# The first batch of a fused retention and mixer kernel: another order of its loads, weight conversions and low parts

## The chip, the cores and the metric

The kernel runs on one core of one Trainium2 chip. The time is the device time of one execution in microseconds (us): 1366.73 is the median of three runs (1365.96 to 1366.76). One more execution was taken with the hardware profiler; it took 1366.12 us. All rows below are from that one.

## The reference

Three stages follow one another, in float32 and float64 (the weights of the mixers come as float64):

```python
# 8 batches, 8 heads, 576 positions, 64 channels a head
scores = scale * np.matmul(q, k.transpose(0, 1, 3, 2))
Dmat = np.where(rel >= 0, gamma[:, None, None] ** rel[None, :, :], 0.0)   # rel = i - j
x = np.matmul(scores * Dmat[None], v)            # heads joined: (8, 576, 512)

h = x.transpose(0, 2, 1) @ U @ V                 # U: 576 x 32, V: 32 x 576
u = x + h.transpose(0, 2, 1)
x = u + np.maximum(u @ w_ch1, 0.0) @ w_ch2       # w_ch1: 512 x 2048

xk = mu_k * x + (1.0 - mu_k) * x_prev            # x_prev: one token earlier
xr = mu_r * x + (1.0 - mu_r) * x_prev
k = np.maximum(xk @ w_k, 0.0)
out = sigmoid(xr @ w_r) * (k * k @ w_v)
```

The change touches the first stage of the first batch, the mixing with U and V, and the preparation of `w_ch1`.

## The kernel before, in words

**Retention.** It goes batch by batch, `NC` = 5 steps each, of 128 positions (the last of 64). A step works on one or two chunks of 64 positions. `scores(i)` multiplies q and k inside each chunk, `decay(i)` weighs the result on VectorE (tile `pm`), `own(i)` multiplies by v. `gain(i)` multiplies k by v to a state per head, `states(i)` adds it to the running state (tiles `w_1`, `w_2`, ...), and `inter(i)` multiplies q by that state. `from_state(i)` weighs the latter (tile `y`), and `leave(i)` adds the two parts into `xt`, the transposed x of the batch. `scale_k` weighs k on GpSimd before its use. Two PSUM pairs, `up` and `dn`, take all these small matmuls, 64 by 64 each. A batch's steps are numbered on: step 5 is the first of the second batch.

**Mixing.** `natural` transposes a step's x back on TensorE (`xn`), ScalarE copies it (`xs`), `low_rank` multiplies it by U (tile `ust`) into `gall`, and `low_rank_sum` makes from the sum over five steps a high part, a low part and a copy of the high part (tile `gt`). `mix` multiplies by V (tile `vst`, which holds a high part twice and a low part) and VectorE adds the product to `xt`. `mix_store` splits the result into high and low parts (`uh`, `ul`) for the dense products.

**Dense products.** `hidden_part` multiplies the mixed x by `w_ch1`. The matmuls are in fp32r, so both factors are split: high by high, high by low, low by high are summed, twelve matmuls of 128x512 for one product (tiles `h_0`, `h_1`, ...). The weight has four column quarters (`w1[0]` to `w1[3]`, in profile names `w_0` to `w_3`), and four products in turn use one quarter. `FIRST` and `FULL` say how many products follow each step.

**Weight conversions.** float64 arrives as two 32-bit words. `convert` makes of it in stages: a load; `down`, a scaling of the upper word on ScalarE (tile `ca`); `fill`, three VectorE instructions that join the words to a float32 (tile `cf`); `split`, a cast to the high part on ScalarE, then a subtraction for the low part, on GpSimd. A quarter is converted in four blocks of 128 rows.

**What sets the order.** Inside `manual_schedule` (L1074) each engine runs its instructions in the order in which the code issues them; an instruction that waits holds up everything behind it on that engine. The stages of conversions are put by hand: `place` takes a conversion's stages and files them in `early` under half-steps (2i is the first half of step i), and `stages` issues what is filed there. Loads go through SyncE's queue in the order of issue.

The lines in the rows: scores L801, `decay` L815, `inter` L834, `own` L853, `gain` L875, `states` L898 and L900, `from_state` L912, `leave` L929, `natural` L939 and L949, `low_rank` L960, `low_rank_sum` L975 to L982, `mix` L990 and L994, dense products L336 with their relu at L342, conversions L104 (ScalarE), L110, L114, L119 (VectorE), L127 (cast) and L128 (low part).

Of the kernel before, what the change touches and what calls it, by code (L numbers as in the profile page):

```python
# [19 lines left out]
DM = H * D  # L20
# [19 lines left out]
def retention_mixer_kernel(ctx: ExitStack, tc: tile.TileContext, io):  # L40
# [90 lines left out]

    waiting, going = [], []
# [13 lines left out]
    class Weight:  # L146
# [9 lines left out]
        def convert(self, pool, raw_pool):  # L156
            for k in range(4):
# [11 lines left out]
                waiting.append(convert(fetch, parts, 128, 512))  # L169


# [560 lines left out]
    with ExitStack() as st:  # L732
# [77 lines left out]
        def decay(i):  # L810
            b, p, cs = chunks(i)
            n = len(cs)
            t = up[i - 1] if i else up.pop(-1)
# [75 lines left out]
        def states(i):  # L889
# [12 lines left out]
            if i == 0:  # L902
                down.pop(-1)
# [31 lines left out]
        def natural(b, p):  # L935
            c0, n = CH[p]
            ps = bank("n", f"xn{b}_{p}")
# [33 lines left out]
        def low_rank_sum(b):  # L971
            gs = small(F32, "gs")[:32]
            gt = a2.tile([96, DM], F32R, tag="gt", name=f"gt{b}")
# [6 lines left out]
            eng = nc.gpsimd if b else nc.vector  # L980
            eng.tensor_tensor(gt[32:64], gs, gt[0:32].bitcast(F32), op=ALU.subtract)
            nc.scalar.copy(gt[64:96], gs)  # L982
            gst[b] = gt
# [3 lines left out]
        def mix(b, k, s):  # L987
# [3 lines left out]
                ps[:, :n], gst[b][:, k * 128:(k + 1) * 128], vst[:, o:o + n], start=True, stop=True  # L991
# [40 lines left out]
        def prep_u():  # L1032
            full, m = (NC - 1) * C, (NC - 1) * RANK
            n = S - full
            raw = []

            def fetch():
                raw.append(big.tile([128, NC * RANK], I64, tag="unit", name="uraw"))
                nc.sync.dma_start(
                    raw[0][:, :m].rearrange("p (c r) -> p c r", r=RANK),  # L1040
                    io["moe_U"][:full].rearrange("(c p) r -> p c r", p=C),
                )
                nc.sync.dma_start(raw[0][:n, m:], io["moe_U"][full:])
                return raw[0][:, :m]

            waiting.append(convert(fetch, lambda: (ust[:, :m], None), 128, m))
            waiting.append(convert(lambda: raw[0][:n, m:], lambda: (ust[:n, m:], None), n, RANK))

        def prep_v():
            q = S // 4
            vh, vl = small(F32R, "vh")[:, :q], small(F32R, "vl")[:, :q]

            def fetch():
                raw = big.tile([128, q], I64, tag="unit", name="vraw")
                for i in range(4):
                    nc.sync.dma_start(raw[32 * i:32 * i + 32], io["moe_V"][:, i * q:i * q + q])
                return raw

            def spread():
                for i in range(4):
# [43 lines left out]
        for w in w1:  # L1106
            w.convert(big, big)
# [434 lines left out]
```

## Time and profile before

| | us |
|---|---|
| median of three runs | 1366.73 |
| lowest, highest | 1365.96, 1366.76 |
| profiled execution | 1366.12 |
| its span (first to last instruction) | 1364.3 |

The page of the profile gives each engine's busy time as a share of the span, and the costliest groups of instructions. The trace behind it is asked by window (busy time of each engine in a stretch of time), by waits (what ended an engine's idle time) and as a timeline (one line for each instruction or run of like instructions, with its start). PE is TensorE, PEld its weight loads, DVE VectorE, ACT ScalarE, POOL GpSimd, SP SyncE. Times in a row are microseconds from the start of the span, unless they are marked ns. In brackets stands how long an engine waited before the instruction, and on what.

### The profile page before, as it was taken

Reading aid. Unit: us, or ns where it says so; the run is one execution under the profiler, and the core shown is the slowest. Engines: PE = TensorE matmul, PEld = TensorE weight load, DVE = VectorE, ACT = ScalarE, POOL = GpSimd, SP = SyncE. Lnnn points to the kernel's source line nnn. Section 1 sums busy time; section 2 is a strip of 40 time slices with the busy share of each in tenths; the row PEclk is TensorE's granted clock in tenths of the full one; section 3 lists DMA queues with packets and bytes.
Section 4 is the critical chain, followed back from the end, with each engine's and each line's share of the span. In section 5 each row is a group of like instructions: output and inputs, shape, how many; then the busy total and the mean of one; then the engine's idle time right before and its main releaser. Section 6 shows DMA issues by size and latency. Waiting matters only on the chain.

```text
span 1364.3 us, 25990 instructions
## 1 busy us (share of the span) xinstructions
PE 1336.9 (98%) x10296; PEld 1099.6 (81%) x10296; DVE 928.6 (68%) x1267; ACT 626.5 (46%) x1089; POOL 369.7 (27%) x301
## 2 busy tenths in 40 slices
PE   6899999999999999999999999999999999999998
PEld 4688887888877888788888888888888888888897
DVE  4893554441432266989798898697787787787753
ACT  4452434343333354544444544465465465465431
POOL 2351333323122155023221222203303303304212
PEclk8799999999999999999999999999999999999999
DMA  9576687886664557969788796786075175174271
GB/s 339 205 261 227 230 296 252 292 301 228 218 211 164 198 194 240 304 197 321 248 297 293 238 321 216 253 310 247 19 287 188 35 274 185 53 271 139 82 306 76
DMA packets 122763, 307.64 MB, mean 225 GB/s; under 512 B 15120, under 2 KB 27792, under 8 KB 122640
## 3 DMA queue, kind: packets, MB, share of 16 engines
q1 hardware_dynamic: 122640, 305.96, 64.4%
q8 instruction: 81, 1.33, 0.4%
q14 instruction: 42, 0.34, 0.1%
HBM read 214.69 MB, written 91.23 MB: 224 GB/s over the span
## 4 chain that ended last, share of the span: by engine, by line
PE 91%; DVE 3%; DMA 3%; issue 2%; ACT 1%; SPq 0%; POOL 0%; DVEq 0%; ACTq 0%
PE h L336 28%; PE v L1387 14%; PE ga L521 5%; PE gc L521 5%; PE gd L521 5%; PE kc L1291 4%; PE kd L1291 4%; PE ka L1291 4%; PE gb L521 3%; PE rd L1291 2%; PE kb L1291 2%; PE rc L1291 2%; PE ra L1291 2%; PE xn L939 2%; DMA rb<-hp 2%
## 5 line engine op out<-in xcount | busy, mean ns | idle before, releaser
L342 ACT ACTIVATE hs<-h 128x512 f32<-128x512 f32 x144 | 86.0, 598 | 233.1 <-PE h L336 228.1
L1343 POOL TENSOR_TENSOR vl<-m,vh 128x512 fp32r<-128x512 f32 (+1 forms) x40 | 47.6, 1192 | 310.2 <-ACT vh L1342 240.2
L815 DVE TENSOR_TENSOR pm<-up,dtab 128x512 f32<-128x512 f32 (+1 forms) x40 | 25.4, 634 | 113.0 <-PE up L801 107.2
L480 ACT CAST sbh<-rb 128x1024 fp32r<-128x1024 f32 x64 | 67.4, 1054 | 59.1 <-PE gd L521 47.4
L481 DVE TENSOR_TENSOR sbl<-rb,sbh 128x1024 fp32r<-128x1024 f32 x64 | 85.4, 1334 | 5.0 <-ACT sbh L480 4.8
L1387 PE MATMUL v<-vh,wv_0u 128*128 128x512 f32 x288 | 88.7, 389 | 0.0
L1387 PE MATMUL v<-vh,wv_1u 128*128 128x512 f32 x288 | 88.7, 389 | 0.0
L481 DVE TENSOR_TENSOR sal<-ra,sah 128x1024 fp32r<-128x1024 f32 (+1 forms) x64 | 65.5, 1023 | 21.5 <-PE gd L521 13.5
L480 ACT CAST sah<-ra 128x1024 fp32r<-128x1024 f32 (+1 forms) x64 | 53.5, 837 | 50.7 <-DVE ra L462 17.9
L763 POOL TENSOR_TENSOR kv<-kv,ktab 128x512 f32<-128x512 f32 (+1 forms) x40 | 42.1, 1051 | 102.3 <-DMA kv<-in_kv 93.2
L1343 POOL TENSOR_TENSOR vl<-c,vh 128x512 fp32r<-128x512 f32 (+1 forms) x40 | 62.2, 1573 | 25.9 <-ACT vh L1342 25.9
L1387 PEld LDWEIGHTS v<-vh,wv_1u 128*128 128x128 f32 x288 | 54.1, 188 | 11.2
L1387 PEld LDWEIGHTS v<-vh,wv_0u 128*128 128x128 f32 x288 | 53.9, 188 | 11.0
L994 DVE TENSOR_TENSOR xt<-mx,xt 128x256 f32<-128x256 f32 x64 | 28.7, 457 | 49.9 <-PE mx L990 49.9
L1342 ACT CAST vh<-m 128x512 fp32r<-128x512 f32 (+1 forms) x40 | 23.2, 579 | 75.3 <-DVE m L1341 75.3
L1387 PE MATMUL v<-vl,wv_0u 128*128 128x512 f32 x144 | 56.0, 389 | 0.0
L1387 PE MATMUL v<-vl,wv_1u 128*128 128x512 f32 x144 | 56.0, 389 | 0.0
L565 POOL TENSOR_TENSOR x<-x,ur 128x512 f32<-128x512 f32 x16 | 24.7, 1556 | 108.0 <-DVE x L561 76.7
L634 ACT ACTIVATE tp<-x2l,omu 128x511 f32<-128x511 f32 x72 | 51.0, 713 | 2.6 <-DMA x2l<-xb 2.6
L538 POOL TENSOR_TENSOR m<-m,ur 128x512 f32<-128x512 f32 x8 | 12.3, 1555 | 133.1 <-ACT m L535 133.1
L1341 DVE SCALAR_TENSOR_TENSOR m<-m 128x512 f32<-128x512 f32 (+1 forms) x40 | 44.8, 1119 | 1.4
L1291 PE MATMUL kc<-kht,wk 128*128 128x512 f32 (+1 forms) x160 | 45.5, 368 | 0.0
(289 smaller groups left out, 3828.2 us busy)
## 6 DMA issues: line engine op xcount, KB each, us to landing
wk<-keys SPq DMA_DIRECT2D x80, 512.0 KB, 5.9
hp<-hs SPq DMA_DIRECT2D x128, 256.0 KB, 3.0
rb<-hp SPq DMA_DIRECT2D x64, 512.0 KB, 5.6
wr<-gates SPq DMA_DIRECT2D x40, 512.0 KB, 7.7
qk<-in_qk SPq DMA_DIRECT2D x32, 512.0 KB, 6.2
kv<-in_kv SPq DMA_DIRECT2D x32, 512.0 KB, 6.9
ra<-hp SPq DMA_DIRECT2D x32, 512.0 KB, 6.8
ur<-ub SPq DMA_DIRECT2D x18, 512.0 KB, 6.1
```

Source lines behind the costliest of these rows:

```text
L336: nc.tensor.matmul(hps[t, f], w.part(lo, k, fo), u[k // 2][:, k % 2, :], start=(part == 0 and k == 0), stop=(part == 2 and k == KD - 1),)
L342: nc.scalar.activation(h, hps.pop((t, f)), AF.Relu)
L480: nc.scalar.copy(hi_, src)
L481: nc.vector.tensor_tensor(lo_, src, hi_.bitcast(F32), op=ALU.subtract)
L521: nc.tensor.matmul(group[g][p], l[:, col(p)], r, start=(h == 0 and j == 0 and i == 0), stop=(i == 2 and last), skip_group_check=True,)
L634: nc.scalar.activation(tp[:, 1:], x[:, :BT - 1], AF.Copy, scale=omu[:, j, k:k + 1])
L763: nc.gpsimd.tensor_tensor(k, k, ktab[:, p, :n].to_broadcast([128, n, NP, D]), op=ALU.mult)
L994: nc.vector.tensor_tensor(u, ps[:, :n], u, op=ALU.add)
L1291: nc.tensor.matmul(ps[b], l, r[:, i], start=(part == 0 and i == 0 and j == 0), stop=(i == 1 and j == 2), skip_group_check=True,)
L1341: nc.vector.scalar_tensor_tensor(x, x, 0.0, x, op0=ALU.max, op1=ALU.mult)
L1343: eng.tensor_tensor(l, x, h.bitcast(F32), op=ALU.subtract)
L1387: nc.tensor.matmul(vacc[t][o], w.part(lo, g, col(o)), x[:, i, :], start=(g == 0 and i == 0 and j == 0), stop=(g == NG - 1 and i == 1 and j ...
```

## The change

- **Loads.** q,k and v of steps 2, 3 and 4 are issued earlier in SyncE's queue, the identity in between, U and V behind step 3 and 4; the first quarter of `w_ch1` behind them. U and V are laid out on the host in the order in which the kernel keeps them, so that each is one transfer, and U is one conversion, not two.
- **The first quarter.** It is converted in four pairs of half-columns: two row blocks by 256 columns each, so that a pair is one `ca` and one `cf` tile, filled and split as one. Pairs 0 and 1 are converted beside the steps, pair 2 behind the batch's last sum; the fourth (pair 3) comes in the dense work.
- **Low parts.** Those of `w_ch1` (the whole weight) are made on VectorE, not on GpSimd; the third block of `vst` is made by four short VectorE subtractions.
- **The end of the first batch.** The last two sums, and then the transposes of steps 3 and 4, stand ahead of scores and gains of the next batch; `low_rank_sum` of the first batch is done in two halves. `inter` and `own` of step 5, scores and gains of step 6 stand behind the first dense product.

On VectorE and ScalarE, at the end of the first batch (steps 3 and 4). VectorE before: `xt` rows are sums of `leave`, `cf` rows are conversions of the first quarter.

```order
L929 TENSOR_TENSOR xt_289<-dn_548,y_575 128x4x128
L110 TENSOR_SCALAR cf<-ca 128x512
L114 SCALAR_TENSOR_TENSOR cf<-ca,cf 128x512
L119 SCALAR_TENSOR_TENSOR cf<-w_0_raw_303,cf 128x512
L110 TENSOR_SCALAR cf<-ca 128x512
L114 SCALAR_TENSOR_TENSOR cf<-ca,cf 128x512
L119 SCALAR_TENSOR_TENSOR cf<-w_0_raw_404,cf 128x512
L815 TENSOR_TENSOR pm_682<-up_632,dtab 128x512
L912 TENSOR_TENSOR y_684<-up_632,qtab 128x4x64
L900 TENSOR_TENSOR w_1_688<-dn_641,w_0_686 128x256
L929 TENSOR_TENSOR xt_289<-dn_641,y_684 128x4x64
```

VectorE now, from the same sum to the conversion of pair 2:

```order
L989 TENSOR_TENSOR xt_299<-dn_551,y_578 128x4x128
L168 TENSOR_TENSOR w_0l_611<-cf,w_0h_610 128x2x256
L972 TENSOR_TENSOR y_640<-up_622,qtab 128x4x64
L989 TENSOR_TENSOR xt_299<-dn_631,y_640 128x4x64
L1142 TENSOR_TENSOR vst<-vf,vh 32x144 x4
L149 TENSOR_SCALAR cf<-ca 128x512
L153 SCALAR_TENSOR_TENSOR cf<-ca,cf 128x512
```

Two conversions, a decay and a state sum stood between the last two sums; a low part (`w_0l`) and the weighing `y` stand there now, and the conversion follows.

ScalarE now, the stretch that leads to the high part `w_0h_610`, of which that low part is made:

```order
L1009 COPY xs_2_599<-xn_2_594 128x512
L1135 CAST vh<-vf 128x144
L1137 CAST vst<-vh 32x144
L1138 CAST vst<-vh 32x144
L1137 CAST vst<-vh 32x144
L1138 CAST vst<-vh 32x144
L1137 CAST vst<-vh 32x144
L1138 CAST vst<-vh 32x144
L1137 CAST vst<-vh 32x144
L1138 CAST vst<-vh 32x144
L167 CAST w_0h_610<-cf 128x2x256
L141 ACTIVATE ca<-w_0_raw_224 128x256
```

Before, the eight copies of V stood between the same two kinds of rows, with the cast of V further ahead and the low part on GpSimd.

On TensorE, around the first dense product `h_0`. Before, the small matmuls of step 5 and what stands behind them (the first mixing product closes the piece; seven more and then `h_0` follow):

```order
L834 MATMUL up_745<-qk_0_412,w_0_686 64x64 x8
L853 MATMUL dn_754<-pm_682,kv_0_414 64x64 x16
L801 MATMUL up_745<-qk_1_526 64x64 x16
L875 MATMUL dn_754<-kv_1_528 64x64 x16
L990 MATMUL mx_0_0_803<-vst,gt_737 128x256
```

Now, from the last mixing product on:

```order
L1067 MATMUL mx_3_1_749<-vst,gt_1_720 128x320
L398 MATMUL h_0_777<-uh_0_752,w_0h_517 128x512 x2
L398 MATMUL h_0_777<-uh_1_753,w_0h_610 128x512 x2
L398 MATMUL h_0_777<-uh_0_752,w_0l_518 128x512 x2
L398 MATMUL h_0_777<-uh_1_753,w_0l_611 128x512 x2
L398 MATMUL h_0_777<-ul_0_754,w_0h_517 128x512 x2
L398 MATMUL h_0_777<-ul_1_755,w_0h_610 128x512 x2
L896 MATMUL up_805<-qk_0_314,w_0_772 64x64 x8
L915 MATMUL dn_814<-pm_770,kv_0_316 64x64 x16
L863 MATMUL up_805<-qk_1_426 64x64 x16
L937 MATMUL dn_814<-kv_1_428 64x64 x16
L398 MATMUL h_1_874<-uh_0_752,w_0h_517 128x512 x2
```

The four groups of small matmuls (`inter`, `own`, scores, `gain`) stood ahead of the mixing and now stand between the first two dense products.

On VectorE in the dense work now, ahead of the fifth dense product, which is the first that reads `w_1h` and `w_1l`:

```order
L119 SCALAR_TENSOR_TENSOR cf<-w_1_raw_422,cf 128x512
L110 TENSOR_SCALAR cf<-ca 128x512
L114 SCALAR_TENSOR_TENSOR cf<-ca,cf 128x512
L119 SCALAR_TENSOR_TENSOR cf<-w_1_raw_424,cf 128x512
L877 TENSOR_TENSOR pm_1104<-up_1038,dtab 128x512
L962 TENSOR_TENSOR w_6_1106<-dn_1055,w_5_977 128x256
L962 TENSOR_TENSOR w_7_1108<-dn_1055,w_6_1106 128x256
L972 TENSOR_TENSOR y_1110<-up_1038,qtab 128x512
L989 TENSOR_TENSOR xt_871<-dn_1055,y_1110 128x4x128
L128 TENSOR_TENSOR w_1l_1020<-cf,w_1h_1019 128x512 x2
```

Before, the same low parts were on GpSimd:

```order
L763 TENSOR_TENSOR kv_3_729<-kv_3_729,ktab 128x2x256
L128 TENSOR_TENSOR w_1l_873<-cf,w_1h_872 128x512
L128 TENSOR_TENSOR w_1l_907<-cf,w_1h_906 128x512 x2
L763 TENSOR_TENSOR kv_4_918<-kv_4_918,ktab 128x256
```

The last two low parts of the second quarter now stand behind two conversions and the five sums of step 7, in VectorE's queue; on GpSimd only the scalings of k stood beside them.

The diff, cut to its core:

```diff
+    def convert_pair(raws, parts):
...
+        def down():
+            got["a"] = cv.tile([128, 512], F32, tag="ca", name="ca", bufs=2)
+            for i in range(2):
+                nc.scalar.activation(
+                    got["a"][:, i * 256:i * 256 + 256], words(i)[:, :, 1].bitcast(F32),
+                    AF.Copy, scale=DOWN,
+                )
+        def fill():
...
+            for i in range(2):
+                x = f[:, i * 256:i * 256 + 256].bitcast(U32)
+                nc.vector.scalar_tensor_tensor(
+                    x, words(i)[:, :, 0], 29, x,
+                    op0=ALU.logical_shift_right, op1=ALU.bitwise_or,
+                )
+        def split():
+            h, l = parts()
+            f = got["f"].rearrange("p (k n) -> p k n", n=256)
+            nc.scalar.copy(h, f)
+            nc.vector.tensor_tensor(l, f, h.bitcast(F32), op=ALU.subtract)
...
-                waiting.append(convert(fetch, parts, 128, 512))
+                waiting.append(convert(fetch, parts, 128, 512, eng=nc.vector))
...
         def low_rank_sum(b):
+            if b == 0:
+                for j in range(2):
+                    gt = a2.tile([96, DM], F32R, tag="gt", name=f"gt{b}_{j}")
+                    for i in range(2):
...
+                        nc.scalar.copy(gt[0:32, o], g)
+                        gst[b, k] = gt
+                    for i in range(2):
...
+                        nc.vector.tensor_tensor(
+                            gt[32:64, o], g, gt[0:32, o].bitcast(F32), op=ALU.subtract
+                        )
+                    o = slice(j * 256, (j + 1) * 256)
+                    nc.scalar.copy(gt[64:96, o], gt[0:32, o].bitcast(F32))
+                return
...
             def spread():
+                nc.scalar.copy(vh, got["f"])
+                for r, s in quarters():
                     nc.scalar.copy(vst[0:32, s], vh[r].bitcast(F32))
                     nc.scalar.copy(vst[32:64, s], vh[r].bitcast(F32))
-                    nc.gpsimd.tensor_copy(vst[64:96, s], vl[r].bitcast(F32))
...
+            def rest_of_v():
+                for r, s in quarters():
+                    nc.vector.tensor_tensor(
+                        vst[64:96, s], got["f"][r], vh[r].bitcast(F32), op=ALU.subtract
+                    )
...
+        get_first, halves_of_first = w1[0].convert_halves(big, big)
+        for (down_, fill_, split_), at in zip(halves_of_first, ((3, 3, 4), (5, 5, 6), (7, 8, 8.2), (10, 10, 11))):
...
-            (0, 5), (1, 6), (2, 7), (3, 8), (5, 10), (6, 11), (7, 11), (8, 12),
+            (1, 11), (2, 12), (3, 13), (3, 13),
...
+        load_to(3)
+        nc.sync.dma_start(ident, io["ident"])
         stages(0)
-        nc.sync.dma_start(ident, io["ident"])
+        load_to(4)
+        stages(0.5)
+        load_to(5)
...
+        for k in range(KD):
+            get_first(k)
...
-        FIRST, FULL = (2, 2, 2, 2, 1, 2, 2, 3), (3, 3, 4, 4, 2)
+        FIRST, FULL = (2, 1, 2, 2, 2, 2, 2, 3), (3, 3, 4, 4, 2)
...
         def step_of(i):
...
             if i == NC:
+                hidden(1, False)
+                stages(10)
+            inter(i)
+            own(i)
+            last = p == NC - 1
+            if b == 0 and last:
+                from_state(i)
+                leave(i)
+                stages(8)
+                low_rank(0, 2)
+                natural(0, 3)
+                natural(0, 4)
+                stages(8.2)
+                next_products(i)
+                low_rank(0, 3)
+                low_rank(0, 4)
+                low_rank_sum(0)
+                later(0)
+                stages(9)
                 mixes(9)
+                next_leaves(i)
+                return
...
```

## Rows read from the trace of the kernel before

**Rows 1.** The page: busy time, share of the span, instructions.

```profile
PE 1336.9 (98%) x10296; PEld 1099.6 (81%) x10296; DVE 928.6 (68%) x1267; ACT 626.5 (46%) x1089; POOL 369.7 (27%) x301
```

**Rows 2.** Windows: length, busy PE, PEld, DVE, ACT, POOL (instructions), clock, DMA share, GB/s.

```profile
40.00:50.00 10.00, 7.49 (x132) 5.15 (x132) 6.08 (x13) 5.44 (x12) 3.51 (x3) 0.67 0.13 53
...
60.00:70.00 10.00, 10.00 (x203) 8.33 (x196) 9.83 (x12) 5.16 (x10) 7.56 (x6) 1.00 0.80 251
```

**Rows 3.** TensorE's waits, 0 to 50: waiter, releaser, sum, count, longest.

```profile
PE up L834 <- issue: 3.0, 1, 3.0
...
PE up L801 <- issue: 1.9, 1, 1.9
```

**Rows 4.** Timeline, TensorE, steps: start, duration, instruction, [wait before, releaser].

```profile
17.38 1.13 PE L875 MATMUL dn<-kv 64*64 64x64 f32 x32 [0.43 <-POOL kv L763]
```

**Rows 5.** Timeline, ScalarE, 29 to 34 us.

```profile
29.67 0.59 ACT L949 COPY xs<-xn 128x512 f32<-128x512 f32 x1 [2.03 <-PE xn L939]
30.47 0.31 ACT L1065 CAST vst<-vh 32x144 fp32r<-32x144 f32 x1
...
32.73 0.62 ACT L127 CAST w_0h<-cf 128x512 fp32r<-128x512 f32 x1
```

**Rows 6.** Timeline, TensorE and VectorE, from the last sum to dense work.

```profile
36.95 0.65 PE L960 MATMUL gall<-xs,ust 128*32 128x128 f32 x8 [0.67 <-ACT xs L949]
...
39.37 0.41 DVE L929 TENSOR_TENSOR xt<-dn,y 128x256 f32<-128x256 f32 x1
39.92 1.03 PE L939 MATMUL xn<-ident,xt 128*64 128x128 f32 x4 [2.32 <-DVE xt L929]
...
43.59 1.08 PE L801 MATMUL up<-qk 64*64 64x64 f32 x32
44.44 1.05 PE L875 MATMUL dn<-kv 64*64 64x64 f32 x32
...
46.42 0.62 PE L990 MATMUL mx<-vst,gt 96*128 96x256 f32 x3 [0.93 <-DVE gt L981]
...
50.06 2.21 PE L336 MATMUL h<-uh,w_0h 128*128 128x512 f32 x4 [0.67 <-DVE xt L994]
```

**Rows 7.** Timeline, TensorE in dense work.

```profile
55.48 1.14 PE L336 MATMUL h<-uh,w_0h 128*128 128x512 f32 x4
...
58.37 0.69 PE L834 MATMUL up<-qk,w 64*64 64x64 f32 x32
...
60.81 1.18 PE L336 MATMUL h<-uh,w_0h 128*128 128x512 f32 x4
...
63.65 1.07 PE L336 MATMUL h<-uh,w_0h 128*128 128x512 f32 x4
```

**Rows 8.** Timeline, VectorE in dense work.

```profile
52.64 0.69 DVE L815 TENSOR_TENSOR pm<-up,dtab 128x512 f32<-128x512 f32 x1
...
55.28 0.42 DVE L110 TENSOR_SCALAR cf<-ca 128x512 uint32<-128x512 uint32 x1
...
56.46 0.69 DVE L119 SCALAR_TENSOR_TENSOR cf<-w_raw,cf 128x512 uint32<-128x512 uint32 x1
57.07 0.42 DVE L110 TENSOR_SCALAR cf<-ca 128x512 uint32<-128x512 uint32 x1
...
61.61 0.68 DVE L815 TENSOR_TENSOR pm<-up,dtab 128x512 f32<-128x512 f32 x1
...
64.19 0.42 DVE L110 TENSOR_SCALAR cf<-ca 128x512 uint32<-128x512 uint32 x1
```

**Rows 9.** Groups by line, VectorE, 50 to 100: busy, mean ns | idle before.

```profile
L119 DVE SCALAR_TENSOR_TENSOR cf<-w_raw,cf 128x512 uint32<-128x512 uint32 x12 | 13.2, 1102 | 0.4
```

**Rows 10.** Timeline, ScalarE, the relu of the first dense product.

```profile
55.72 0.60 ACT L342 ACTIVATE hs<-h 128x512 f32<-128x512 f32 x1 [0.81 <-PE h L336]
```

**Rows 11.** A TensorE wait in dense work (timeline), and the window behind it.

```profile
208.06 1.19 PE L336 MATMUL h<-uh,w_2h 128*128 128x512 f32 x4 [1.81 <-ACT hs L342]
...
209.00:213.00 4.00, 4.00 (x38) 2.73 (x40) 1.81 (x3) 0.38 (x2) 0.00 (x0) 0.57 0.32 119
```

More of the change, by code (lines that the diff above doesn't have):

```diff
@@ L1046, in prep_u @@
[L1046 to L1047 removed]
+                raw = big.tile([128, NC * RANK], I64, tag="unit", name="uraw")
+                nc.sync.dma_start(raw, io["moe_U"])
+                return raw
+            waiting.append(convert(fetch, lambda: (ust, None), 128, NC * RANK))
         def prep_v():
             q = S // 4
[L1053 removed]
+            vh = small(F32R, "vh")[:, :q]
@@ L1055, in fetch, with parts, quarters @@
+            got = {}
             def fetch():
                 raw = big.tile([128, q], I64, tag="unit", name="vraw")
-                for i in range(4):
-                    nc.sync.dma_start(raw[32 * i:32 * i + 32], io["moe_V"][:, i * q:i * q + q])
-                return raw
+                nc.sync.dma_start(raw, io["moe_V"])
+                return raw
+            def parts():
+                got.setdefault("f", small(F32, "vf")[:, :q])
+                return got["f"], None
+            def quarters():
+                return [(slice(32 * i, 32 * i + 32), slice(i * q, i * q + q)) for i in range(4)]
@@ L1070, in retention_mixer_kernel @@
+            job = convert(fetch, parts, 128, q)
+            waiting.append(job[:3] + [spread, rest_of_v])
         seq = [(b, p) for b in range(B) for p in range(NC)]
@@ L1139, in retention_mixer_kernel @@
         states(0)
-        load_to(4)
         scale_k(0, 1)
+        for k in range(KD):
+            get_first(k)
         def next_qtab(p):
@@ L1147, in next_qtab, with plan, next_products @@
                 )
-        due, first = {}, {}
+        due = {}
         quiet = []
-        def plan(i, fn, *args, where=due):
-            where.setdefault(i, []).append((fn, args))
-        FIRST, FULL = (2, 2, 2, 2, 1, 2, 2, 3), (3, 3, 4, 4, 2)
-        def products_of(i):
-            inter(i)
-            own(i)
+        def plan(i, fn, *args):
+            due.setdefault(i, []).append((fn, args))
+        FIRST, FULL = (2, 1, 2, 2, 2, 2, 2, 3), (3, 3, 4, 4, 2)
+        def next_products(i):
             if i + 1 < N:
@@ L1197, in step_of @@
                 next_qtab(i + 1)
-            for fn, args in due.pop(i, []):
+            for fn, args in sorted(due.pop(i, []), key=lambda x: x[0] is natural and b == 0):
                 fn(*args)
```

121 lines of the change are left out of this document (73 added, 48 removed).

## The prediction

> **What bounds the kernel now.** The page comes first: TensorE is busy for 98% of the span [rows 1], so a change gains only where TensorE waits or where work on it disappears. The change removes no matmul, so what counts is the time at which the dense products start and whether TensorE waits afterwards. The windows say where it waits: in 40 to 50 us it is busy 7.49 of 10 us, from 60 us on it is full while VectorE beside it is 98% busy [rows 2]. So the head has idle time to win, and the stretch behind it has no spare VectorE time to lose. The list of TensorE's waits in the first 50 us then tells who holds it: its two long "issue" waits, 3.0 and 1.9 us, name no engine and no transfer [rows 3]. The only wait in the loop of steps that a late load can be blamed for is one on GpSimd's scaling of k, 0.43 us [rows 4]. The timeline, last, gives the end of the head: at 39.37 us VectorE writes the last sum of the first batch, then come transposes, low-rank products, mixing, and the first dense product at 50.06 [rows 6].
>
> **The change, part by part.** All times are of the profiled execution.
>
> *q, k, v first.* In SyncE's queue k,v of step 2 stands four issues earlier. The price of that lateness was the 0.43 us above; the rest of the first 30 us is the loop of sums and small matmuls and the "issue" waits, which the change leaves in place. I take 0. The ends: nothing, and all 4.9 us of the two waits [rows 3], should they be due to the traffic of the loads.
>
> *The last sum of the first batch comes earlier, but behind ScalarE.* The two conversions that stood directly in front of it on VectorE are gone from there. In their place stands the low part of pair 1, ahead of the last step's two sums, and that needs ScalarE's cast of the high part, which stands behind the copy of the transposed step 2, the cast of V and eight copies of V. Today the transposed copy starts at 29.67; the next step has one more low-rank group ahead of it (0.5), so it ends at about 30.8. The cast and eight copies, nine at 0.31 or a little more, and the cast of 0.62 [rows 5] bring 34.3. Low part 0.7 (0.69 is what a VectorE instruction of this size with two operands in SBUF takes, [rows 8]), two half-width sums of 0.41: the last sum ends at 35.8 instead of 39.78. From there TensorE does the transpose (1.03), scores and gains of the next batch (43.59 to the end of the group begun at 44.44, 1.9, at the clock of that stretch), and two low-rank groups (0.65 each, overlapping: 1.2): 40.0 [rows 6]. The new low-rank sum needs two short copies and two short subtractions before the first mixing product; at the 0.31 us of a 32-partition copy that is 1.2: 41.2. Mixing took 46.42 to 50.06, 3.6 us [rows 6], and has 0.6 us of subtractions of the second half in front of its sums now: dense work starts at 45.5, **4.6 us earlier**. Converting pair 2 in between is hidden by scores, gains and low-rank groups: four copies of V's low part and the conversion end near 39. The ends for this term are -9.5 (all issue waits gone too) and -2.5 (GpSimd's scalings hold VectorE up twice by 1 us).
>
> *Four groups of small matmuls change sides.* inter, own, scores and gains of step 5 ran before 50.06; now they stand behind the first dense product. At full clock such a set with four transposes takes 58.37 to 60.81 [rows 7], 2.4 us, without the transposes 2.0: **+2.0**. They filled a wait before, so this is a real cost.
>
> *Clock.* The first dense product took 50.06 to 55.48, 5.4 us, the third 2.8 [rows 7]: 2.6 us lost at the half clock. It may be lost again, or not at all; on the other side one wait of 1.81 us in dense work was followed by 4 us at a mean clock of 0.57 [rows 11], some 1.7 us. Middle of -2.6 and +1.7: **-0.5**.
>
> *Low parts on VectorE, and the fourth pair in dense work.* Count from the start of dense work, VectorE's queue in its order. Today it is done with mixing and starts decay at +2.6 (52.64) [rows 8]; with one state sum it is free at +3.7. Next stands the conversion of pair 3, which needs ScalarE's two scalings, and these stand behind the relu of the first dense product: that ends at +5.4, relu 0.6 [rows 10], scalings 0.7: +6.8, so VectorE waits 3 us. Conversion of a pair as long as that of a row block, 55.28 to 57.07, 1.8 [rows 8]: +8.6. Five sums with half-width output, 52.64 to 55.28, 2.6: +11.2. Its low part waits for a cast behind the second relu: +12.4. Then conversion 1.8, five sums 61.61 to 64.19 2.6 [rows 8], low part 0.6, conversion 1.8, low part 0.6, two conversions 3.6, five sums 2.6, two low parts 1.3: **+27.3**. The last two low parts are what the fifth dense product (first of the second weight quarter) reads from its seventh matmul on. TensorE gets there after 5.4 + 2.0 + 2.8 + 2.4 + 2.8 + 2.8 + 2.8 = 21.0 and 1.4 for six matmuls: +22.4. TensorE waits **5 us**, some of it already at the groups of steps 6 and 7, whose sums come late. In the kernel before, the same low parts were made on GpSimd directly behind the casts, without five sums and three conversions in front of them. The ends: 0.7 us, if none of ScalarE's waits is seen, and 7 us, if two scalings of k hold VectorE for a further us each.
>
> *Third and fourth weight quarter.* The last cast of each stands on ScalarE right behind the relu of the product just finished, and the next product reads it in its third matmul: relu 0.6 and cast 0.6 [rows 5, 10] and 0.1 between them, less 0.45 for two matmuls, 0.9 us each. For the fourth, the second batch's low-rank copies (some 2.8 us) stand there too; I take 1.8. Together **+2.7**, between 0 and 5.
>
> **Sum:** -4.6 + 2.0 - 0.5 + 5.0 + 2.7 = +4.6. The profiled execution took 1366.12 (span 1364.3); the median of the three runs, 1366.73, lies 0.6 above it. 1366.7 + 4.6 = 1371.3.
>
> **A rule weighed.** Undisturbed conversions take 1.8 us, yet the twelve third instructions average 1.10 us instead of 0.69 [rows 8, 9]: they stretch while GpSimd works. The Trainium skill (SBUF — State Buffer, "SBUF: two separate sides") says that VectorE and GpSimd share a pair of ports, held for a whole instruction by whoever starts first while the other stands still. The trace agrees. It speaks for the change: low parts on VectorE take most of GpSimd's holds away. By the rule alone the added low parts, twelve of 0.69, are about paid for by the stretch that goes, some 11 us over 36 instructions. My tally already uses undisturbed times, so the rule does not lower the 5 us: what makes them is the order of the queue.
>
> **The rivals.**
> *Faster: VectorE is ahead all the same.* It was 98% busy from 60 us on and TensorE did not wait [rows 2]. If relus and casts never hold it, and the low parts of the second quarter land before +22.4, the two waits vanish: -4.6 + 2.0 - 0.5 = -3.1, 1363.6. From 3.1 us of waits on, it is no gain. Against it stands the tally: VectorE's own instructions alone end at +23.1, 20.5 us of them from +2.6 on. Chance 0.18.
> *No change.* Half of the waits, 4 of 7.7 us, are seen, or the "issue" waits of the head shrink because U and V come in one transfer each: 4.6 less 3 to 6. About 1366. Chance 0.18. The Trainium skill (Runtime: NRT & Kernel Launch, "Instruction fetch mechanics") has instructions fetched ahead at almost no cost. The trace has waits of 3.0 and 1.9 us in which nothing is waited for; if they are not the fetch, they may go, and this is the case.
> *Much slower: the clock falls in the waits.* As at 208.06 [rows 11], each wait of 2 us may be followed by some 4 us at about half clock, 1.7 us each. Three more of these (second, third and fourth quarter) less what VectorE's lateness hides anyway: 1375 to 1377. Chance 0.14.
> *The change does not do what it says:* "q, k, v first" gains nothing, since no load is late by more than 0.43 us. That is in the forecast.
>
> **How the numbers follow.** The forecast, waits of 5 to 10 us against 3 us won, has 0.50; its own range is 1368 to 1375. No change can be told within 0.2%, 2.7 us. Slower by more: 0.50 and 0.14, less a little for its lower edge, 0.62. Within: 0.19. Faster by more: the faster case, and the best ends of the no-change case: 0.19. The best ends together (-9.5, -2.6, 0.7, 0, with +2.0) would give 1357, the worst 1380; I leave out a tenth on each side: 1362.5 to 1377.
>
> **What would show it.** Right: the first dense matmul at 44.5 to 47 us; ScalarE's eight copies of V still between the transposed copy and the cast in 30 to 34.5, with VectorE waiting for the cast; in 60 to 80 us a TensorE wait of some us on VectorE's low part or ScalarE's cast before the fifth dense product, and short ones before the ninth and thirteenth; GpSimd idle there; conversions near 1.8 us each. Wrong: TensorE 10.00 of 10 in every window from 50 to 110 us (then the faster case), or a head whose "issue" waits are under 1 us, or dense work that starts after 48.

## The result and the profile after

The changed kernel takes 1376.99 us (median of four runs, 1374.91 to 1378.04), the kernel before 1366.74 on the same chip. The ratio is 1.0074, with a 95% interval of 1.0056 to 1.0091: slower by some 10 us. The forecast was slower by 4.6. The time lies above the 1368 to 1375 of the forecast itself, on the figures of the rival "much slower" and just inside the upper end of the whole range, 1377. The profiled execution took 1376.88, span 1375.1.

Relus are the same 144 in both kernels, so their starts make a ledger. The first starts 1.77 us earlier than before (53.95 against 55.72), the fifteenth 13.19 later (127.81 against 114.62), the 28th still 13.19, the 41st 10.74, the last ones 10.13. So the head wins 1.8, the first 80 us of dense work lose 15.0, and the rest gives 3.1 back. Between starts of products on TensorE the loss divides so:

| stretch | before | after | difference |
|---|---|---|---|
| up to the first dense product | 50.06 | 48.29 | -1.77 |
| first product | 5.42 | 5.55 | +0.13 |
| groups of step 5 (before: in the head) | | 1.82 | +1.82 |
| second product, groups of step 6 | 5.33 | 5.86 | +0.53 |
| third, fourth, groups of step 7 | 8.44 | 10.88 | +2.44 |
| fifth, sixth, groups of step 8 | 7.76 | 13.07 | +5.31 |
| seventh to twelfth, steps 9 to 11 | 25.40 | 25.40 | 0.00 |
| thirteenth, groups of step 12 | 5.60 | 10.28 | +4.68 |

The windows of the changed kernel (columns as in [rows 2]), and behind them two more of the kernel before:

```profile
40.00:50.00 10.00, 5.67 (x32) 3.45 (x29) 8.53 (x18) 5.19 (x12) 1.11 (x1) 0.67 0.06 22
60.00:70.00 10.00, 8.20 (x240) 6.66 (x231) 8.56 (x15) 4.22 (x8) 0.91 (x1) 1.00 0.80 257
70.00:80.00 10.00, 7.29 (x25) 4.39 (x24) 9.14 (x17) 3.37 (x6) 1.04 (x1) 0.89 0.52 193
110.00:120.00 10.00, 7.32 (x128) 5.23 (x129) 5.45 (x8) 3.17 (x6) 2.23 (x2) 0.83 0.13 45
```

```profile
70.00:80.00 10.00, 10.00 (x127) 8.05 (x126) 9.79 (x15) 4.07 (x8) 4.68 (x4) 1.00 0.91 322
110.00:120.00 10.00, 10.00 (x130) 8.18 (x129) 3.94 (x8) 3.35 (x5) 1.04 (x1) 1.00 0.29 110
```

TensorE, full before in the last three of these windows, now idles 1.8, 2.7 and 2.7 us in them, and GpSimd is nearly empty: its low parts are gone. In 110 to 120 us VectorE has spare time in both kernels (busy for 3.94 and 5.45 of 10 us), and yet TensorE now waits there. In 40 to 50 TensorE is busy less than before (5.67 against 7.49), with VectorE busier.

The head, timeline of ScalarE, VectorE and TensorE; it answers to [rows 5] and [rows 6]:

```profile
30.86 0.59 ACT L1009 COPY xs<-xn 128x512 f32<-128x512 f32 x1 [2.54 <-PE xn L999]
...
34.27 0.62 ACT L167 CAST w_0h<-cf 128x512 fp32r<-128x512 f32 x1
```

```profile
34.92 1.21 DVE L168 TENSOR_TENSOR w_0l<-cf,w_0h 128x512 fp32r<-128x512 f32 x1 [3.20 <-ACT w_0h L167]
36.06 0.41 DVE L972 TENSOR_TENSOR y<-up,qtab 128x256 f32<-128x256 f32 x1
36.57 0.42 DVE L989 TENSOR_TENSOR xt<-dn,y 128x256 f32<-128x256 f32 x1
37.02 2.00 DVE L1142 TENSOR_TENSOR vst<-vf,vh 32x144 fp32r<-32x144 f32 x4
39.05 0.43 DVE L149 TENSOR_SCALAR cf<-ca 128x512 uint32<-128x512 uint32 x1
...
42.41 0.69 DVE L168 TENSOR_TENSOR w_0l<-cf,w_0h 128x512 fp32r<-128x512 f32 x1 [0.68 <-ACT w_0h L167]
43.13 0.59 DVE L1043 TENSOR_TENSOR gt<-gall,gt 32x128 fp32r<-32x128 f32 x2
```

```profile
37.05 1.06 PE L999 MATMUL xn<-ident,xt 128*64 128x128 f32 x4 [3.87 <-DVE xt L989]
...
39.96 0.91 PE L1020 MATMUL gall<-xs,ust 128*32 128x128 f32 x16
43.56 0.90 PE L1067 MATMUL mx<-vst,gt 96*128 96x256 f32 x3 [2.69 <-DVE gt L1043]
...
48.29 2.21 PE L398 MATMUL h<-uh,w_0h 128*128 128x512 f32 x4 [0.68 <-DVE xt L1071]
```

Two waits stand in series. VectorE waits 3.20 for the cast of pair 1, which ScalarE reaches only behind nine copies of V. Then TensorE has its low-rank sum at 40.87 and waits 2.69 more, because VectorE does four V subtractions (2.00), the conversion of pair 2 (39.05 to 41.72) and, after 0.68 of wait for ScalarE's cast, its low part first.

Dense work, timeline of TensorE (the rows with a wait):

```profile
69.48 0.33 PE L999 MATMUL xn<-ident,xt 128*128 128x128 f32 x1 [1.60 <-issue]
...
73.76 1.05 PE L398 MATMUL h<-uh,w_1h 128*128 128x512 f32 x2 [0.74 <-ACT w_1h L127]
...
77.08 1.28 PE L398 MATMUL h<-uh,w_1l 128*128 128x512 f32 x2 [1.81 <-DVE w_1l L128]
...
112.94 0.50 PE L398 MATMUL h<-uh,w_3h 128*128 128x512 f32 x1 [1.23 <-ACT w_3h L127]
...
115.61 0.79 PE L398 MATMUL h<-uh,w_3l 128*128 128x512 f32 x1 [1.45 <-DVE w_3l L128]
```

The first of them ends on nothing that the profile shows ("issue"); it is called a wait without a releaser below. Behind the third and the last of them the clock falls to its lower level, 1.2 GHz (windows):

```profile
78.00:81.00 3.00, 3.00 (x41) 2.07 (x44) 1.38 (x2) 0.90 (x2) 0.00 (x0) 0.50 0.00 0
116.00:118.00 2.00, 2.00 (x5) 1.09 (x4) 0.00 (x0) 0.00 (x0) 0.00 (x0) 0.50 0.00 0
```

VectorE, the low parts that the fifth product waits for, and what stands ahead of the thirteenth's, with ScalarE's cast for the latter:

```profile
76.23 1.39 DVE L128 TENSOR_TENSOR w_1l<-cf,w_1h 128x512 fp32r<-128x512 f32 x2
...
110.47 1.77 DVE L119 SCALAR_TENSOR_TENSOR cf<-w_raw,cf 128x512 uint32<-128x512 uint32 x1
112.16 0.68 DVE L877 TENSOR_TENSOR pm<-up,dtab 128x512 f32<-128x512 f32 x1
112.27 0.62 ACT L127 CAST w_3h<-cf 128x512 fp32r<-128x512 f32 x1 [0.26 <-DVE cf L119]
...
114.87 0.68 DVE L128 TENSOR_TENSOR w_3l<-cf,w_3h 128x512 fp32r<-128x512 f32 x1
```

For the thirteenth, ScalarE's cast ended at 112.89, yet the low part came at 114.87: the five sums of a step stood between.

Most of what came back later is a clock drop that the kernel before had and this one has not. At 208.06 TensorE waited 1.81 for a relu, and the clock was 0.57 behind it [rows 11]. The same wait is 1.48 here (at 220.33), with the clock full:

```profile
219.00:223.00 4.00, 2.67 (x12) 2.17 (x12) 2.20 (x5) 2.31 (x5) 0.00 (x0) 1.00 0.69 272
```

The ledger moves by 1.9 us there (12.60 to 10.74). Another 1.1 (11.16 to 10.10) comes back at 395.02, where the kernel before waits 0.86 without a releaser and this one does not. The first of the two needs none of the moved work: the version below that changes the load order alone has no such drop either (its ledger goes from 2.44 to 0.38 there).

### The profile page after: what moved, and what is told of

Its sections match the earlier page's. It is cut to its first block, busy times and chain, and to the rows that moved or that the text cites. A ratio compares the mean times of both kernels' runs of the same rounds, so it can differ in the third digit from the quotient of the medians.

```text
span 1375.1 us, 25970 instructions
## 1 busy us (share of the span) xinstructions
PE 1340.4 (97%) x10296; PEld 1099.8 (80%) x10296; DVE 935.7 (68%) x1290; ACT 626.7 (46%) x1092; POOL 344.3 (25%) x281
## 4 chain that ended last, share of the span: by engine, by line
PE 88%; DVE 5%; issue 1%; ACT 1%; DMA 1%; SPq 0%; DVEq 0%; ACTq 0%
PE h L398 26%; PE v L1490 14%; PE gc L583 6%; PE gd L583 6%; PE ga L583 6%; PE kd L1394 4%; PE kc L1394 4%; PE ka L1394 4%; PE gb L583 3%; PE rd L1394 2%; PE rc L1394 2%; PE kb L1394 2%; PE ra L1394 2%; PE xn L999 1%; PE up L896 1%; PE c L665 1%
```

## Experiments

Times are medians on a chip with runs of the kernel before; the ratio is against that kernel. "The ledger" is the shift of a relu against the kernel before, in the one profiled execution of each.

**Low parts back on GpSimd.**

```diff
-                waiting.append(convert(fetch, parts, 128, 512, eng=nc.vector))
+                waiting.append(convert(fetch, parts, 128, 512))
```

> The changed kernel with the low parts of the second to fourth weight quarter back on GpSimd, nothing else. Theory A (order of the queues): the fifth and thirteenth dense product wait because the last casts of a quarter stand behind a relu on ScalarE and behind conversions and sums on VectorE; moving the low parts alone shortens the waits for a low part (1.81 and 1.45 us) by about half, leaves those for a cast (0.74 and 1.23), and takes 1 to 4 us off 1377. Rival B (the low parts are what is too much for VectorE): both waits vanish with the half clock behind them, and 8 to 10 us go: 1367 to 1369. Rival C (shared port): GpSimd's low parts stretch the conversions by as much as they save, no change within 1 us.

1370.85, ratio 1.0032 (1.0019 to 1.0044): 6.1 less, between theory A's 1 to 4 and rival B's 8 to 10. The ledger at the fifteenth relu is 7.69, not 13.19. Casts are still waited for (0.74, 0.51), low parts less (0.73 and 0.23, on GpSimd), and no half clock follows them. So the low parts in VectorE's queue make somewhat over half of the loss. Rival C fell.

**V's copies ahead.** One more call of `stages` stands between `next_qtab` and the transposes.

```diff
-        place(0.5, 2, 2, 6, 8)
+        place(0.5, 2, 2, 5.5, 8)
...
                 next_qtab(i + 1)
+            if b == 0:
+                stages(2 * i - 0.5)
```

> The changed kernel with ScalarE's nine copies of V issued ahead of the copy of the transposed step 2, in a stretch where ScalarE waits 2.5 us for that transpose; nothing else. Theory A: VectorE's wait of 3.20 us for the cast of pair 1 falls below 1, the last sum of the first batch ends near 34.5 us in place of 36.99, and the first dense product starts 2 to 2.7 us earlier than 48.29; the total falls by about as much, 1374.5 to 1375. Rival: the last sum isn't what the mixing waits for (VectorE's V subtractions and the conversion of pair 2 are): dense work starts less than 0.7 us earlier, the total stays within 1 us.

1371.96, ratio 1.0037 (1.0024 to 1.0050): 5.0 less. VectorE waits 0.49 for the cast, the last sum ends at 33.97, dense work starts at 45.40, 2.9 us earlier. That is a little more than theory A had; but the total fell by 2 us more than the start. The fifth product's wait of 1.81 for the low part is gone here, and at the sixth relu the ledger is 5.71, not 10.64. The trace shows how. Behind the wait without a releaser (1.61 here, 1.60 in the changed kernel) the clock fell this time, 0.50 in 67 to 70 us, and the fourth product took 4.4 us in place of 2.8. So TensorE came to the low part when it was nearly ready, waited 0.15, and no half clock followed there. Why the clock fell behind the one of these two waits and not behind the other stays open.

**Pairs 2 and 3 behind the mixing.** `split` is divided into a cast and a low part.

```diff
-((3, 3, 4), (5, 5, 6), (7, 8, 8.2), (10, 10, 11))
+((3, 3, 4, 4), (5, 5, 6, 6), (7, 9.5, 10, 11), (9, 9.5, 10, 11))
...
                 next_leaves(i)
+                stages(9.5)
                 return
```

> The changed kernel with pair 2 converted behind the mixing, not ahead of the low-rank sum, and pair 3 scaled on ScalarE ahead of the first relu; pair 2 and 3 are first read by the third dense product. Theory A: the wait of 2.69 us before mixing falls to about 1, dense work starts 1.5 to 2 us earlier than 48.29, VectorE's idle 3.35 us behind its mixing work is filled by the two conversions, and the third product does not wait longer: total 1.5 to 2 us less, 1375. Rival B (VectorE has no spare time in dense work): what the head wins comes back as waits before step 6's groups and the third product, total unchanged within 1 us.

1375.24, ratio 1.0059 (1.0046 to 1.0073): 1.75 less, within theory A; but the interval overlaps that of the changed kernel, so the gain is not clear of noise. The wait before mixing is 1.07, now for ScalarE. Dense work starts at 47.54, only 0.75 earlier, since the head's own waits were longer in this execution (the last transpose starts at 37.61, not 37.05).

**Conversions a half-step earlier.**

```diff
-            (1, 11), (2, 12), (3, 13), (3, 13),
+            (1, 10), (2, 11), (3, 12), (3, 12),
```

and so on to `(16, 20)`.

> The changed kernel with every conversion of the second to fourth quarter placed one half-step earlier, nothing else; the low parts stay on VectorE. Theory A: the waits before the fifth and thirteenth product (5.3 and 4.7 us with the half clock behind them) come from stages that are due half a step too late; most of both goes, total 6 to 9 us less, 1368 to 1371. Rival B (VectorE has too much to do): the waits move to the groups of small matmuls in front of them, which wait for the sums, and less than 3 us go.

1371.28, ratio 1.0033 (1.0021 to 1.0045): 5.7 less, just under theory A's 6 to 9. No dense product waits for a weight any more. But rival B is half right: step 6's and 7's groups wait for VectorE's sums instead, and the wait without a releaser grew (TensorE, timeline):

```profile
60.51 0.69 PE L896 MATMUL up<-qk,w 64*64 64x64 f32 x32 [2.17 <-DVE y L972]
...
66.75 0.84 PE L896 MATMUL up<-qk,w 64*64 64x64 f32 x32 [0.76 <-DVE y L972]
...
72.91 0.33 PE L999 MATMUL xn<-ident,xt 128*128 128x128 f32 x1 [2.98 <-issue]
```

**Parts of the change alone, in the kernel before.** Low parts of all quarters on VectorE:

```diff
-                waiting.append(convert(fetch, parts, 128, 512))
+                waiting.append(convert(fetch, parts, 128, 512, eng=nc.vector))
```

> The kernel before with one part of the change alone: low parts of all four quarters on VectorE. Theory A: VectorE's sum of work stays about the same (sixteen low parts of 0.69, 11 us, against conversions that get shorter by about as much), but each low part stands behind a cast on ScalarE, so the sums come later: 1 to 4 us slower, as waits of the small matmuls for the sums. Rival B (too much for VectorE): 6 us or more slower. Rival C (the shorter conversions pay for all): within 1 us.

1372.93, ratio 1.0047 (1.0035 to 1.0059): 7.2 slower, nearest to rival B's 6 or more. Most of it is in the head, where the ledger is +4.63 at the first relu: the low parts of the first quarter hold up VectorE's sums and the low-rank sum, the latter with a wait of 2.81 before mixing. Dense work adds 2.5, of which 1.9 is one wait without a releaser. Theory A named the mechanism and missed its size.

Loads of q, k, v of steps 2 to 4 ahead of U, V and the weights:

```diff
+        load_to(3)
+        nc.sync.dma_start(ident, io["ident"])
+        load_to(4)
+        load_to(5)
         stages(0)
-        nc.sync.dma_start(ident, io["ident"])
...
-            load_to(i + 4)
+            load_to(i + (4 if i >= NC else 5))
```

> The kernel before with the other part alone: q,k and v of steps 2 to 4 loaded ahead of U, V and the first quarter. Theory A (the prediction's zero): no load but one of 0.43 us is waited for, and the waits without a releaser do not depend on it: within 1 us of before. Rival: the waits without a releaser in the head (6.2 us in all) shrink, or a late U or weight adds a wait: 2 us or more either way.

1366.33, ratio 1.0001 (0.9992 to 1.0010): no change in total, as the prediction took it. In its profiled execution the first relu comes 1.92 later than before, and the last one 0.42, since the clock drop at 208 us is missing. One execution of each does not show whether the head itself is longer.

**The four edits together**, with the first block of the second quarter left at `(1, 11)`:

> The changed kernel with four edits together: V's copies ahead of the transposed step 2, pairs 2 and 3 converted behind the mixing, conversions of the later quarters a half-step earlier (that of the second quarter's first block as it was), low parts of these quarters on GpSimd. Theory A: each edit takes away a wait of its own in the head (about 3 and 1 to 1.5 us), the last two share the waits before the fifth and thirteenth product (6 to 8 together): dense work starts near 44 us, no dense product waits over 0.5 us for a weight, 1361 to 1365. Rival: VectorE's sums, behind earlier conversions, hold up the small matmuls by 4 us or more: 1366 to 1368.

1364.96, ratio 0.9987 (0.9977 to 0.9996). Dense work starts at 41.46, 8.6 us earlier than before, and no product waits for a weight. The time is at the end of theory A's range, and yet only 0.8 us under the runs of the kernel before beside it, since most of the head is lost again: the ledger goes from -7.39 at the third relu to +2.08 at the fifth. Between them stands the wait at the transposes of step 7, now the largest, with half clock behind it, and a wait for the sums as the rival has it:

```profile
58.19 0.88 PE L900 MATMUL up<-qk,w 64*64 64x64 f32 x32 [1.89 <-DVE y L976]
...
65.73 0.48 PE L1003 MATMUL xn<-ident,xt 128*128 128x128 f32 x1 [4.35 <-issue]
65.86 2.06 PE L402 MATMUL h<-uh,w_0h 128*128 128x512 f32 x4
```

The same without the last edit, low parts on VectorE:

> The same without the last edit: low parts of the later quarters stay on VectorE. Theory A (VectorE's queue is what is late): the small matmuls' waits for the sums grow by 3 us or more against the version with GpSimd, 1364 to 1368. Rival (with the stages early enough, the low parts cost nothing, since conversions beside an idle GpSimd are shorter by as much): the same as the version with GpSimd within 1 us.

1365.25, ratio 0.9991 (0.9982 to 1.0000): the same within 1 us. The rival holds: once the stages are early enough and the head is clear, the low parts on VectorE cost nothing that can be told. Theory A's 3 us fell.

**What the wait without a releaser is.** 40 TensorE instructions more in the warm-up (ten long matmuls in place of twelve, 22 short ones added), in the changed kernel and in the version with four edits:

```diff
-WARM = 12
+WARM = 10
...
+        for i in range(22):
+            nc.tensor.matmul(
+                turn("u", ("n", "g"), f"warm{WARM + i}")[:, :64],
+                warm[:, 0, :], warm[:, 0, 0:64], start=True, stop=True,
+            )
```

> The changed kernel with 40 more TensorE instructions in the warm-up (two long matmuls less, 22 short ones more) and nothing else. TensorE's wait without a releaser at the transposes of step 7 (1.60 us, and 4.35 in the version with four edits) stands at the same place of the program in both. Theory A: it is a wait for TensorE's next instructions, which come in blocks of a fixed number of instructions through the same transfer engines as the weights, so the place moves 40 instructions ahead, the block before it is entered in the third dense product instead of at the start of step 7's groups, and the wait at the transposes goes: total 1 to 2 us less, 1375 to 1376. Rival: it belongs to the transposes or to what stands there; the wait stays within 0.5 us.

> The version with four edits, and the same 40 instructions more. Theory A: the wait of 4.35 us at the transposes of step 7 goes, and the half clock behind it (about 2.5 us): 1358 to 1360. Rival: the wait stays, or VectorE's sums and weights take its place: over 1363.

1378.38 (ratio 1.0085, 1.0065 to 1.0104) and 1371.87 (1.0032, 1.0019 to 1.0045): both slower, not faster. The waits, TensorE's timeline of the one and of the other:

```profile
68.39 0.38 PE L937 MATMUL dn<-kv 64*64 64x64 f32 x9 [1.94 <-issue]
```

```profile
34.72 0.33 PE L919 MATMUL dn<-pm,kv 64*64 64x64 f32 x3 [1.57 <-issue]
...
68.06 0.58 PE L941 MATMUL dn<-kv 64*64 64x64 f32 x9 [3.86 <-issue]
```

The wait moved from ahead of the last transpose to ahead of the last 9 matmuls of `gain`. Nine matmuls, eight of the low-rank group and three transposes lie between, each with a weight load: 40 instructions, exactly the number added. So it stands at a count of instructions, and the rival fell. That the wait would go fell too: it is about as long as before (1.94 against 1.60, 3.86 against 4.35). But it is not what made the two slower. At the fifteenth relu the ledger of the first is 9.57, less than the changed kernel's 13.19. It loses near 270 us, at a new wait of the same kind, and so does the second, whose head is longer as well (dense work starts at 45.26, not 41.46):

```profile
273.43 0.50 PE L398 MATMUL h<-uh,w_1h 128*128 128x512 f32 x1 [2.54 <-issue]
```

```profile
268.30 1.88 PE L402 MATMUL h<-uh,w_1h 128*128 128x512 f32 x4 [3.00 <-issue]
```

Behind both the clock is at 0.50 for 3 us, and the ledgers go from 7.25 to 11.73 and from 2.36 to 7.27. The two versions without the 40 instructions have no wait there. So the added instructions moved more than the one place that they were meant for, and these totals do not price that one wait.

**Two products between steps 6 and 7:**

```diff
-        FIRST, FULL = (2, 1, 2, 2, 2, 2, 2, 3), (3, 3, 4, 4, 2)
+        FIRST, FULL = (2, 2, 2, 2, 1, 2, 2, 3), (3, 3, 4, 4, 2)
```

> The version with four edits, with two dense products instead of one between the groups of step 6 and 7 (the table of the kernel before). Theory A: the block of instructions in question is entered in the product and ends in step 7's groups, as in the kernel before, which did not wait there; and VectorE gets 2.7 us more for the sums that step 7 waits for (1.89 us): both waits go, 1357 to 1360. Rival: the fifth product now comes before its weights and waits 2 us or more: 1362 or over.

1361.20, ratio 0.9957 (0.9942 to 0.9973): 6.0 us under the runs of the kernel before beside it. The wait for the sums is gone, and the ledger stays below zero all the way. The wait without a releaser is 2.52, ahead of the last matmul of `gain`, so theory A was half right. The instruction queue (q8, 81 packets in the whole run) carries one packet in 62.00 to 62.25; TensorE goes on at 64.58.

**Sixteen instructions more ahead of the mixing:**

```diff
                 stages(9)
+                filler = bank("n", "filler")
+                for _ in range(8):
+                    nc.tensor.matmul(
+                        filler[:, :64], warm[:, 0, :], warm[:, 0, 0:64], start=True, stop=True
+                    )
                 mixes(9)
```

> The version with four edits and two products between steps 6 and 7, with 16 TensorE instructions more that no result uses (8 short matmuls and their weight loads) ahead of the mixing of the first batch, where TensorE waits 1.08 us anyway. There the wait without a releaser (2.52 us) ended in step 7's groups, with the block of instructions asked for where these groups begin (59.97) and carried at 62.0, behind a burst of loads. Theory A: 16 instructions more move the request into the fourth dense product, near 58.3 us, ahead of that burst; the wait goes, and the half clock behind it (about 1.6 us): 1357 to 1358.5. Rival: the block is carried no earlier, or the wait stands elsewhere with the same length: 1360.5 or over.

1360.14, ratio 0.9958 (0.9941 to 0.9974): no different from the version before it. The wait moved 16 instructions ahead and fell to 0.57, the half clock behind it is gone, and the packet came at 61.00 to 61.25, as step 7's groups begin (61.23); in the version before it came 2 us behind their start (59.97). It still came amid a stretch of full transfers (share 0.91 in 60 to 62), not ahead of it. From the start of these groups to that of step 8's it is 11.09 us now, 12.90 there. Two things take most of the gain. Step 7's groups begin 1.26 later, since dense work starts at 43.03, not 42.48, and its first product is longer at the lower clock; and the fifth product now reaches its weights before they are there (0.57 for the cast, 0.70 for the low part):

```profile
63.79 0.35 PE L941 MATMUL dn<-kv 64*64 64x64 f32 x9 [0.57 <-issue]
...
66.35 0.50 PE L402 MATMUL h<-uh,w_1h 128*128 128x512 f32 x1 [0.57 <-ACT w_1h L127]
...
68.25 0.50 PE L402 MATMUL h<-uh,w_1l 128*128 128x512 f32 x1 [0.70 <-POOL w_1l L128]
```

## Why the prediction was right in sign and short in size

The sign came out, and so did its reason: waits in dense work that cost more than the head wins. The size did not, 10 us for 4.6. That the time still lies in the range is luck, by 0.01 us; and one of the signs named for being wrong, dense work that starts after 48, came true (48.29). In the ledger the head missed by 2.8, the third and fourth quarter by 2.0, 3.0 stood nowhere in the sum, and 3.1 came back.

- **"q, k, v first ... I take 0."** Right in the total. But the waits without a releaser, which "the change leaves in place", did not stay: in the loop of steps they come to 3.0 us, 6.2 before, while TensorE waits 3.9 us there for VectorE's `y`, 0.7 before, and step 3's sum starts at 31.03, not 29.23. One reading was wrong: the 0.43 us is not the only wait for the scaling of k; in the kernel before the first step waits 1.72 for it as well. Nothing hangs on it, since that matmul starts at 7.76 there and at 7.79 now.
- **The head, 4.6 us won.** It won 1.8. The step that failed is "Converting pair 2 in between is hidden": TensorE's low-rank sum was there at 40.87, 0.9 behind the tally, and 2.69 us of wait followed where 1.2 were counted. V's subtractions took 0.50 each, not the 0.31 of a copy on ScalarE; the conversion of pair 2 took 2.7, not 1.8, beside a scaling on GpSimd (39.62 to 41.10); and pair 2's low part with its wait for the cast, 1.4, stood in no tally. Mixing took 4.7, not 4.2. The 0.9 is the last sum, at 36.99 and not 35.8: the copy of step 2 began 0.7 later than I had it, and the low part took 1.21 beside GpSimd's scaling, not 0.7. Clearing both queues moved the start to 41.46.
- **Four groups change sides, +2.0.** 1.82.
- **Clock, -0.5 as a middle.** The first product lost its half clock again (5.55 us). The third of the rivals had the other half: two waits in dense work were each followed by about 3 us at the lower level. At the rate of undisturbed products and groups (2.7 for twelve matmuls, 2.1 for step 8's groups) this costs 2.1 and 1.6. In the prediction this was 0.14 of the chance, and its time, 1375 to 1377, is the one measured; but it counted three such waits, and the two here make 3.7 of the 10 us, so the agreement is in part luck.
- **VectorE's queue before the fifth product, 5.0.** Right in place; that the size fits, 5.31 with step 8, is luck. The tally put the last low part at 27.3 after the start of dense work; it ended at 29.3. The waits are shorter than 5 (0.74 and 1.81), since TensorE came to the fifth product 24.1 after that start, not 21.0, with 1.6 us of wait without a releaser in it; the half clock, which the term leaves out, made up the sum. (VectorE's own instructions in this tally add up to 21.0 us, not 20.5; nothing hangs on it.)
- **Third and fourth quarter, 0.9 and 1.8.** The ninth product waited 0.51, and the stretch around it lost nothing. The thirteenth lost 4.68. I had only the cast behind the relu in the sum. Its VectorE conversion was late as well (1.77 for its third instruction, beside GpSimd's own work at 110.40 and 111.77), and the low part stood behind the five sums of step 12, the very pattern I had worked out for the fifth product and not applied here. For the fourth quarter that is 4.7 in place of 1.8, a miss as large as the head's. Nor was it VectorE's load: the 98% read off 60 to 70 us does not hold there, it was busy 3.94 of 10 us before.
- **Not in the sum at all:** 1.60 us at step 7's transposes and what it carried with it (+2.44), 0.5 around the second product, and 3.1 us given back later, 1.9 of them one clock drop that did not occur again.
- **The rule weighed.** The third instructions of a conversion average 0.77 us over 60 us of dense work, not 1.10 [rows 9]. The Trainium skill (SBUF — State Buffer, "SBUF: two separate sides") has VectorE and GpSimd lock each other out of a shared pair of ports; the trace agrees. The low parts (12.9 us) and V's subtractions (2.0) that VectorE took over are thereby paid for by two thirds: up to 140 us its conversions take 34.7 us, 44.8 before. And the four edits with low parts on VectorE against those on GpSimd (1365.25, 1364.96) show them costless where order leaves them room. In the changed kernel's order, though, moving them back was worth 6 us. "What makes them is the order of the queue" holds.

```profile
L119 DVE SCALAR_TENSOR_TENSOR cf<-w_raw,cf 128x512 uint32<-128x512 uint32 x11 | 8.5, 773 | 0.4
```

Open stays when TensorE's next block of instructions is asked for; no run shows the moment that the expectations take for it. In the twelve kernels with such a wait in dense work near 65 to 75 us, TensorE went on 2.0 to 2.7 us after the quarter of a microsecond in which the packet was carried. In the version with two products it came at the end of a stretch of full transfers; in the changed kernel with 40 instructions more it came at 65.75 to 66.00, with no transfers at all in 65.0 to 65.5. So the traffic alone does not explain how late it is, and a run without that traffic was not made.

## What to carry to other kernels

Before moving work to an engine with spare time on average, write down for each moved instruction what stands in front of it in that engine's queue at the place where its reader waits; here the sums and casts in front took longer than the work itself, and half a step in a table of stages was worth as much as the choice of the engine. Do the tally for every place of the same pattern, not for the first alone, and price a long wait of TensorE with the half clock that may follow (here 2.1 and 1.6 us behind two of them). When a head gets shorter, look again at what bounded the stretch behind it: here a wait for instructions at the same place grew from 1.60 to 4.35 us and, with the half clock behind it, took most of what had been won. And when instructions are added to move one such wait, look at the whole run: here they brought a new one near 270 us.

## What the runs showed that was not expected

TensorE can wait for its own program. The waits without a releaser stand at a count of instructions: adding 40 or 16 instructions moved them by 40 and 16. Counted in the traces, 1107 matmuls, each with its weight load, stand ahead of the one in dense work in all eleven versions of the changed kernel, whatever stands around it; the waits in the heads, those of the kernel before among them, stand behind 221, 348, 474 or 475, and 601 matmuls, some 127 apart. The run has 20,592 TensorE instructions (10,296 matmuls, as many weight loads) and 81 packets on the instruction queue, some 254 a packet. A set of four groups of small matmuls is 256 instructions in 2.0 us, a dense product 24 in 2.7, so such a set uses up a packet's instructions in about the 2.0 to 2.7 us that pass after a packet. That this is why waits stand at these groups is argued, not shown: others, 2.54 at 273.43 above and 0.86 at 395.02 before, stand inside dense products. The Trainium skill (Runtime: NRT & Kernel Launch, "Instruction fetch mechanics") calls the crossing of a block mostly hidden. The trace agrees for most of the 81 packets, and not for all: waits of 0.57 to 4.35 us stood at such places, and those of the kernel before are 3.0 and 1.9 [rows 3].
